# A decode step of attention and feed-forward: sixteen partitions of the first w_down load come through GpSimd's DMA queue

## The chip, the cores and the metric

The kernel runs on one core of a Trainium2 chip. The metric is the device time of one execution in microseconds (us), the median of several runs. The kernel before took 408.2 us, the median of three runs that lie between 408.13 and 408.52 us.

## The reference: what is computed

It is one decode step of a transformer layer for one token. All tensors are bfloat16.

```python
x = A_x                                                     # 1 x 1024
h = x + _A_ref(_layernorm(x), A_k_cache, A_v_cache, A_wq, A_wo)
h2 = h + _B_ref(_layernorm(h), B_w_gate, B_w_up, B_w_down)  # the output, 1 x 1024
# _A_ref: q = x @ wq (32 heads of 128); scores against 65536 cached keys of 4 kv heads,
#         softmax, times the cached values, then @ wo
# _B_ref: (gelu(x @ w_gate) * (x @ w_up)) @ w_down          # 1024 -> 3584 -> 1024
```

The token is one row, so every matrix is read once and used once. The inputs together are 173 MB, nearly all of it the caches.

## The kernel before, in words

**The ring.** All large inputs pass through one SBUF buffer, `ring`, of three slots. A slot holds 65,536 bytes in each of the 128 partitions. The helper `load` (L171) picks the next slot when its offset is 0, or a place within the current slot otherwise, and issues one DMA from SyncE's queue (SP, L178). It waits for whoever read that place last. There are 26 such loads: wq, sixteen halves of a head's keys or values, wo, w_gate, two halves of w_up, and five pieces of w_down. A load of 128 partitions of 64 KB each appears in the trace as 128 packets, one for each partition. They run on 16 DMA engines, eight packets on each, and are followed on each engine by a 4-byte packet that counts up the semaphore. A load has landed when all 16 engines have counted.

**The order of the work.** First come layernorm and q, then for each of the four kv heads the scores of the keys (PE, with transposes on DVE), the softmax and the sums over the values, then wo, the second layernorm, w_gate, w_up, the gelu and w_down. The order on PE, DVE and ACT in the attention part is written by hand: `keep` (L135) ties each operation to the one before it on its engine, through `pe`, `dv` and `ac`. The scheduler orders the rest by data.

**The end.** `wd_v` views w_down as 128 partitions of 28 columns, each column 1024 numbers (2 KB) wide; row f of w_down is partition f // 28, column f % 28. The five loads take 14, 7, 4, 2 and 1 columns, one after another in one slot, which is the slot that wo had. For each column, `out_mm` (L490) multiplies the column of `actz` with the 1024 numbers in four matmuls of 256, into the four groups of 32 partitions of the PSUM tile `f_ps`. So PE uses a load as soon as it has landed, and the last load holds a single column. After some loads `keep_busy` runs a few matmuls whose result nobody reads. At the end DVE copies `f_ps` to `o_fin` (L581), and SP writes it out (L582).

**GpSimd (POOL).** It issues no DMA in the kernel before. Late in the kernel it clears `o2z`, `hnz` and `actz` (L236) and then takes the power in the second layernorm (`ln_rstd`, L225).

Of the kernel before, what the change touches and what calls it, by code (L numbers as in the profile page):

```python
# [11 lines left out]
BF16 = mybir.dt.bfloat16  # L12
# [5 lines left out]
def kernel(  # L18
# [13 lines left out]
    nc = tc.nc  # L32
    P = 128
    D = A_x.shape[-1]
# [53 lines left out]
    top = ctx.enter_context(tc.tile_pool(name="top", bufs=1))  # L88
# [46 lines left out]
    def keep(op, eng):  # L135
        ins = op.ins
        if eng in latest:
            tc.add_manual_dep(ins, latest[eng].name,
                              mybir.DependencyInfo(mybir.DependencyClass.NoSync, mybir.DependencyReason.DATA),
                              reason="order")  # L140
        latest[eng] = ins
        return op
# [4 lines left out]
    def dv(op):  # L147
        return keep(op, "dv")

    def ac(op):  # L150
        return keep(op, "ac")

# [15 lines left out]

    slot = [NSLOT - 1]

    def load(src, off=0):  # L171
        n, w = src.shape[1], src.shape[2]
        if off == 0:
            slot[0] = (slot[0] + 1) % NSLOT
        assert off + n * w <= 2 * CW
        o = slot[0] * 2 * CW + off
        tv = ring[:, o:o + n * w].rearrange("p (n w) -> p n w", w=w)
        nc.sync.dma_start(out=tv, in_=src)  # L178
        return tv

    wq_v = A_wq.rearrange("(p c) n -> p c n", c=DC)
# [1 line left out]
    nc.scalar.dma_start(out=x_row[0:97:32, :], in_=A_x[0, 0].rearrange("(g n) -> g n", g=4))  # L183
    assert DC * HD == 2 * CW
    wq_t = load(wq_v[:])

    make_identity(nc, ident_bf[:])
# [12 lines left out]
    for bp in range(4):  # L200
        s0 = 64 * (bp // 2) + bp % 2
        nc.vector.tensor_copy(out=esel[:, bp, :, :],
                              in_=ident_bf[:, s0:s0 + 63:2].unsqueeze(1).to_broadcast([P, 4, 32]))
# [30 lines left out]
    def padded(i, vec, ncols, name):  # L234
        t = pt_tile(i, [P, ncols, 32], BF16, name)
        nc.gpsimd.memset(t[:], 0.0)  # L236
        nc.vector.tensor_copy(out=t[:, :, 0], in_=vec)
        return t
# [40 lines left out]
    def kv_load(what, g, li, n):  # L279
        t = load((k_v if what == "k" else v_v)[g][:, li * LN:(li + n) * LN, :])  # L280
        for u in range(n):
            state[(what, g, li + u)] = t[:, u * LN:(u + 1) * LN, :]
# [22 lines left out]
    def k_keep(g, li):  # L305
        qk_ps = state.pop(("qk", g, li))
        if li == 0:
            state[("mx", g)] = small.tile([P, NL], F32, name="mx", tag="mx")
        flat = qk_ps[:].rearrange("p k n -> p (k n)")
        if li < NL - 1:  # L310
            sc = low.tile([P, 2 * 512], F32, name="sc", tag=f"sc{li}")
            ac(nc.scalar.copy(out=sc[:], in_=flat))  # L312
            state[("sc", g, li)] = sc[:]
        else:
            state[("sc", g, li)] = flat
        dv(nc.vector.tensor_reduce(out=state[("mx", g)][:, li:li + 1], in_=flat, axis=AX.X, op=ALU.max))  # L316
# [22 lines left out]
    def softmax_exp(g, li):  # L339
        st = state[("vs", g)]  # L340
        pT = pt_tile(li, [P, GPL, TG * rep], BF16, "pT")
        flat = pT[:].rearrange("p m c -> p (m c)")
        ac(nc.scalar.activation(out=flat, in_=state.pop(("sc", g, li)), func=ACT.Exp, bias=st["nbias"][:, 0:1],  # L343
                                scale=scale, accum_out=st["lpart"][:, li:li + 1]))
        st["pT"][li] = pT
# [19 lines left out]
    def v_evac(g):  # L365
        st = state[("vs", g)]
        acc = st["acc"]
        acc_sb = low.tile([P, TG * Dh], F32, name="acc_sb", tag="qk")
        for c in range(4):
            sl = slice(32 * c, 32 * c + 32)  # L370
            if c < 2:
                dv(nc.vector.tensor_copy(out=acc_sb[sl, :], in_=acc[sl, c, :]))  # L372
            else:
                ac(nc.scalar.copy(out=acc_sb[sl, :], in_=acc[sl, c, :]))  # L374
        lsum = small.tile([P, 1], F32, name="lsum", tag="lsum")
        dv(nc.vector.tensor_reduce(out=lsum[:], in_=st["lpart"][:], axis=AX.X, op=ALU.add))
        lrow = small.tile([P, rep], F32, name="lrow", tag="lrow")
        dv(nc.vector.tensor_scalar(out=lrow[:], in0=hmask[:], scalar1=lsum[:, 0:1], scalar2=None, op0=ALU.mult))
        st["end"] = acc_sb, lrow
# [88 lines left out]
    def row_bank(name):  # L468
        return ps_w.tile([P, 512], F32, name=name, tag="w")
# [9 lines left out]
    assert Hq * D == 2 * CW  # L479
    at_ps = [row_bank("at_ps") for _ in range(DS)]  # L480
    wv = load(wo_v[:])
    for c in range(Hq):
        row_mm(at_ps, o2z[:, c, :], wv[:, c, :], c, c < 4, c + 4 >= Hq)
# [6 lines left out]
    def out_mm(stat, mov, first, last, groups=range(4)):  # L490
        for g in groups:
            mm(f_ps[32 * g:32 * g + 32, :], stat, mov(g), first, last, tile_position=(0, 32 * g),
               skip_group_check=True)
# [65 lines left out]
        nc.vector.tensor_tensor(out=by_j(act_bf, j0, nj), in0=src, in1=by_j(gl, j0, nj), op=ALU.mult)  # L559

    wd_v = B_w_down.rearrange("(p c) n -> p c n", p=P)
    sizes = [14, 7, 4, 2, 1]
    assert sum(sizes) == FC
    actz = padded(3, act_bf[:], FC, "actz")
    w_ps = row_bank("w_ps")

    def keep_busy(n, src):
        for _ in range(n):
            mm(w_ps[:], ident_bf[:], src, True, True)

    keep_busy(8, wu[:, 0, 0:512])
    busy = [3, 2, 1, 0, 0]
    c0 = 0
    for sz, nb in zip(sizes, busy):
        wv = load(wd_v[:, c0:c0 + sz, :], c0 * D)
        for cc in range(sz):
            c = c0 + cc
            out_mm(actz[:, c, :], lambda g: wv[:, cc, g * OW:(g + 1) * OW], False, c + 1 == FC)
        c0 += sz
        keep_busy(nb, wv[:, 0, 0:512])  # L580
# [32 lines left out]
```

## Time and profile before

The profile is one execution. Its span, from the first to the last instruction, is 406.4 us. No separate time of that execution is recorded; the median of the runs is 408.2 us, so 1.8 us lie around the span.

| | before |
|---|---|
| median of the runs | 408.2 us (408.13 to 408.52) |
| span of the profiled execution | 406.4 us |
| bytes moved, mean rate | 173.19 MB, 426 GB/s |
| PE busy | 297.6 us (73%) |
| DVE busy | 202.2 us (50%) |
| POOL busy | 7.5 us (2%) |
| last w_down load landed | 402.80 us |
| result copied, write issued | 403.18 us, 403.63 us |

The engines are PE (matrix multiply), PEld (its weight loads), DVE (VectorE), ACT (ScalarE), POOL (GpSimd) and SP (SyncE). A line of the timeline has the start in us, the time taken, the engine, the kernel's line, the operation, its output and inputs, the number of instructions, and in brackets how long the engine stood idle before and what ended that. A row "DMA" gives, for 40 equal slices of the stretch asked for, the mean busy share of the 16 DMA engines in tenths.

The trace also holds a record of each DMA packet: its start, length, bytes and queue, but not the number of its engine. Since an engine starts a packet at once when the one before ends, the packets can be strung into 16 series, end to start. The 16 counts of each load's semaphore are in the trace too, with their times.

### The profile page before, as it was taken

To read this page: it belongs to the slowest core of one execution; us is meant where nothing else is said; L and a number is where in the kernel's file an instruction comes from. 1 tells how busy PE (TensorE), PEld (TensorE's weight loads), DVE (VectorE), ACT (ScalarE), POOL (GpSimd) and SP (SyncE) were. 2 spreads that over 40 slices of the span, in tenths; PEclk is the share of its full clock that TensorE was granted. 3 is DMA by queue.
4 is the path that set the end of the run, shared out by engine and by line. 5 is a ranking of instruction groups with operands and counts; after the bars stand their busy time and mean duration, and the time that the engine had idled before them with its cause. 6 is when DMAs were issued, how large, how long until landed. Compare 5 with 4: busy or idle time off the path is not lost.

```text
span 406.4 us, 2649 instructions
## 1 busy us (share of the span) xinstructions
PE 297.6 (73%) x1493; PEld 65.4 (16%) x743; DVE 202.2 (50%) x185; ACT 40.9 (10%) x63; POOL 7.5 (2%) x17
## 2 busy tenths in 40 slices
PE   0160777658799796879979957998795999666283
PEld 0120111111111110131111003111110211312141
DVE  0210978999838743972595397509843000221110
ACT  1000000013000022100000302000031000100000
POOL 2000000000000000000000000000010000000000
PEclk9995589998899999669999968899899699766979
DMA  9999999999999999999999999999999999999995
GB/s 413 413 413 458 471 408 419 413 485 432 419 421 413 484 426 419 427 419 484 413 419 434 426 471 413 419 441 426 458 419 426 440 432 452 414 420 423 429 420 216
DMA packets 3772, 173.19 MB, mean 426 GB/s; under 512 B 424, under 2 KB 432, under 8 KB 688
## 3 DMA queue, kind: packets, MB, share of 16 engines
q1 hardware_dynamic: 3752, 173.02, 98.6%
q8 instruction: 9, 0.15, 0.1%
q14 instruction: 3, 0.02, 0.0%
q10 hardware_dynamic: 8, 0.00, 0.0%
HBM read 173.02 MB, written 0.00 MB: 426 GB/s over the span
## 4 chain that ended last, share of the span: by engine, by line
PE 47%; DMA 30%; DVE 18%; ACT 3%; issue 1%; SPq 0%; ACTq 0%; DVEq 0%
DMA ring<-in_A_k_cache_dram 20%; PE acc_ps L158 18%; DVE ring L291 12%; DMA ring<-in_B_w_down_dram 10%; PE qk_ps L156 10%; PE qk_ps L158 9%; PE acc_ps L156 6%; DVE mx L316 3%; ACT sc L312 2%; DVE pT L349 2%; PE o_ps L156 1%; PE at_ps L156 1%; PE at_ps L158 1%; DVE acc_sb L372 1%; ACT pT L343 1%
## 5 line engine op out<-in xcount | busy, mean ns | idle before, releaser
L291 DVE STREAM_TRANSPOSE ring<-ring 128x2048 uint32<-128x2048 uint32 x64 | 142.5, 2278 | 33.0 <-DMA ring<-in_A_k_cache_dram 32.9
L156 PE MATMUL qk_ps<-ring,wsel 128*128 128x512 bf16 x256 | 108.6, 424 | 48.7 <-DVE ring L291 29.2
L158 PE MATMUL qk_ps<-ring,wsel 128*128 128x512 bf16 x256 | 108.2, 423 | 0.0
L158 PE MATMUL acc_ps<-ring,pT 128*128 128x512 bf16 x384 | 105.7, 385 | 0.0
L156 PEld LDWEIGHTS <-wsel 128*128 128x128 bf16 x256 | 27.3, 107 | 157.2 <-issue 142.9
L156 PE MATMUL acc_ps<-ring,pT 128*128 128x512 bf16 x128 | 49.3, 385 | 0.0
L316 DVE TENSOR_REDUCE mx<-qk_ps 128x1 f32<-128x1024 f32 x16 | 19.5, 1219 | 28.7 <-ACT sc L312 22.5
L349 DVE STREAM_TRANSPOSE pT<-pT 128x1024 bf16<-128x1024 bf16 x16 | 19.3, 1227 | 23.8 <-ACT pT L343 23.8
L156 PEld LDWEIGHTS <-pT 128*128 128x128 bf16 x128 | 12.9, 100 | 91.3 <-issue 91.2
L312 ACT COPY sc<-qk_ps 128x1024 f32<-128x1024 f32 x12 | 12.1, 1012 | 149.2 <-PE qk_ps L158 149.2
L372 DVE COPY acc_sb<-acc_ps 32x512 f32<-32x512 f32 x8 | 5.3, 667 | 30.1 <-PE acc_ps L158 30.0
L343 ACT ACTIVATE pT<-sc,nbias 128x1024 bf16<-128x1024 f32 x12 | 13.7, 1141 | 45.2 <-DVE nbias L335 42.2
L156 PE MATMUL ln_tot<-ln_s,ones_f 128*128 128x1 f32 x8 | 2.1, 337 | 13.4 <-DVE ln_s L209 11.6
L156 PE MATMUL o_ps<-sel,acc_sb 128*128 128x8 f32 x32 | 7.3, 358 | 5.8 <-DVE rl L386 5.4
L156 PE MATMUL q_ps<-ring,xnz 128*32 128x512 bf16 x32 | 4.4, 528 | 8.9 <-DMA ring<-in_A_wq_dram 8.9
L374 ACT COPY acc_sb<-acc_ps 32x512 f32<-32x512 f32 x8 | 4.6, 577 | 59.2 <-DVE acc_sb L372 59.1
L156 PE MATMUL wu_ps<-ring,hnz 128*32 128x512 bf16 x32 | 4.6, 502 | 7.2 <-DMA ring<-in_B_w_up_dram 7.2
L156 PEld LDWEIGHTS o_ps<-sel,acc_sb 128*128 128x128 f32 x32 | 7.0, 324 | 6.0 <-issue 5.1
L156 PE MATMUL wg_ps<-ring,hnz 128*32 128x512 bf16 x32 | 5.1, 577 | 3.9 <-DMA ring<-in_B_w_gate_dram 3.9
L343 ACT ACTIVATE pT<-qk_ps,nbias 128x1024 bf16<-128x1024 f32 x4 | 4.5, 1113 | 29.8 <-PE acc_ps L158 16.8
L156 PE MATMUL f_ps<-ring,actz 128*32 128x256 bf16 x112 | 4.0, 274 | 4.4 <-DMA ring<-in_B_w_down_dram 4.4
L248 DVE COPY q_ev<-q_ps 128x512 f32<-128x512 f32 x1 | 0.7, 691 | 12.9 <-PE q_ps L158 12.9
(105 smaller groups left out, 88.9 us busy)
## 6 DMA issues: line engine op xcount, KB each, us to landing
ring<-in_B_w_gate_dram SPq DMA_DIRECT2D x1, 7168.0 KB
ring<-in_B_w_up_dram SPq DMA_DIRECT2D x2, 3584.0 KB, 37.1
ring<-in_B_w_down_dram SPq DMA_DIRECT2D x1, 3584.0 KB, 36.4
ring<-in_B_w_down_dram SPq DMA_DIRECT2D x1, 1792.0 KB, 39.0
ring<-in_B_w_down_dram SPq DMA_DIRECT2D x1, 1024.0 KB, 40.6
ring<-in_B_w_down_dram SPq DMA_DIRECT2D x1, 512.0 KB
ring<-in_B_w_down_dram SPq DMA_DIRECT2D x1, 256.0 KB, 41.6
ring<-in_A_k_cache_dram SPq DMA_DIRECT2D x8, 38.2
```

Source lines behind the costliest of these rows:

```text
L156: return pe(t.matmul(out, lhsT=lhsT, rhs=rhs, start=start, stop=stop, tile_position=tile_position, skip_group_check=skip_group_check))
L158: op = t.add_instruction(mybir.InstMatmult(name=nc.get_next_instruction_name(), engine=t.engine, start_tensor_calc=start, stop_tensor_calc ...
L248: nc.vector.tensor_copy(out=dst, in_=src)
L291: dv(nc.vector.transpose(out=kt[:, c * w:(c + 1) * w], in_=kt[:, c * w:(c + 1) * w]))
L312: ac(nc.scalar.copy(out=sc[:], in_=flat))
L316: dv(nc.vector.tensor_reduce(out=state[("mx", g)][:, li:li + 1], in_=flat, axis=AX.X, op=ALU.max))
L343: ac(nc.scalar.activation(out=flat, in_=state.pop(("sc", g, li)), func=ACT.Exp, bias=st["nbias"][:, 0:1], scale=scale, accum_out=st["lpart ...
L349: dv(nc.vector.transpose(out=flat, in_=flat))
L372: dv(nc.vector.tensor_copy(out=acc_sb[sl, :], in_=acc[sl, c, :]))
L374: ac(nc.scalar.copy(out=acc_sb[sl, :], in_=acc[sl, c, :]))
```

## The change

The first w_down load of 14 columns becomes two, of 6 and of 8 columns. The one of 6 columns is made by a new function, `load_apart`: SyncE's queue brings partitions 0 to 111, and GpSimd's queue brings partitions 112 to 127 in three loads of 6, 6 and 4 partitions. Ahead of each of these stands a tiny load into a new tile `turn`, 4 bytes in each of 10 partitions, and after the last one a tiny load for 2 partitions. So GpSimd's queue gets seven DMAs, of 10, 6, 10, 6, 10, 4 and 2 partitions. `po` ties them in this order. `load` gets an argument for the number of partitions. The list `busy` gets a 0 for the added load, so the idle matmuls after the first six columns stay three.

```diff
+    def po(op):
+        return keep(op, "po")
...
-    def load(src, off=0):
+    def load(src, off=0, parts=P):
...
-        nc.sync.dma_start(out=tv, in_=src)
+        nc.sync.dma_start(out=tv[0:parts], in_=src[0:parts])
...
-    sizes = [14, 7, 4, 2, 1]
+    sizes = [6, 8, 7, 4, 2, 1]
...
+    turn = top.tile([P, 2], BF16, name="turn")
+
+    LOW, HIGH = 10, 6
+
+    def load_apart(src):
+        tv = load(src, parts=P - 16)
+        at = P - 16
+        for n in (HIGH, HIGH, 16 - 2 * HIGH):
+            po(nc.gpsimd.dma_start(out=turn[0:LOW, :], in_=A_x[0, 0, 0:2 * LOW].rearrange("(p n) -> p n", n=2)))
+            po(nc.gpsimd.dma_start(out=tv[at:at + n], in_=src[at:at + n]))
+            at += n
+        po(nc.gpsimd.dma_start(out=turn[0:2 * HIGH - LOW, :],
+                               in_=A_x[0, 0, 0:2 * (2 * HIGH - LOW)].rearrange("(p n) -> p n", n=2)))
+        return tv
...
-    busy = [3, 2, 1, 0, 0]
+    busy = [3, 0, 2, 1, 0, 0]
...
-        wv = load(wd_v[:, c0:c0 + sz, :], c0 * D)
+        wv = load_apart(wd_v[:, :sz, :]) if c0 == 0 else load(wd_v[:, c0:c0 + sz, :], c0 * D)
```

In the built program POOL issues the first tiny load after it clears `xnz`, at the start of the kernel. It issues the first load of 6 partitions, the second tiny load and the second load of 6 after it clears `actz` and ahead of `ln_rstd` of the second layernorm. The other three DMAs follow `ln_rstd`. SP's order keeps, with one load more.

## The prediction

> **What bounds the kernel now.** I read the page's row of the DMA engines first, then the queues, then the chain of waits near the end, and last the timeline of the last microseconds.
>
> ```profile
> DMA  9999999999999999999999999999999999999995
> ...
> q1 hardware_dynamic: 3752, 173.02, 98.6%
> q8 instruction: 9, 0.15, 0.1%
> q14 instruction: 3, 0.02, 0.0%
> ```
>
> The 16 DMA engines are busy from the first slice to the last; SP's queue (q1) holds them for 98.6% of the span. PE (73%) and DVE (50%) have room. Two other queues carry twelve small packets called "instruction".
>
> ```profile
> 361.22 41.58 DMA ring<-in_B_w_down_dram
> 402.80 0.04 issue
> 402.84 0.32 PE f_ps L156 x4
> 402.84 0.29 PE L156 MATMUL f_ps<-ring,actz 128*32 128x256 bf16 x4 [0.23 <-DMA ring<-in_B_w_down_dram]
> 403.18 0.42 DVE L581 CAST o_fin<-f_ps 97x256 bf16<-97x256 f32 x1 [11.29 <-PE f_ps L156]
> ```
>
> The first three lines are the chain, the others the timeline. PE waits for the last w_down load, which lands at 402.80; four matmuls, a copy and the write out follow, 3.6 us to the span's end at 406.4. Nothing of the change touches that tail, so the time moves with the last landing.
>
> Now the DMA engines between 400 and 403 us, in slices of 0.075 us:
>
> ```profile
> DMA  9759896959492938383734645554920000000000
> ...
> q1 hardware_dynamic: 243, 0.61, 50.8%
> q8 instruction: 1, 0.02, 2.2%
> ```
>
> They don't end together. The share sinks for over a microsecond before it is 0. The semaphore counts of the last load give it exactly: six engines land within 0.31 us of the first (400.82), one at +0.64, nine from +1.33 to +1.98. The mean of the 16 is 1.06. In the load that lands at 21.8 us all 16 lie within 0.53 us. The packet series show where the lateness comes from. A 64 KB packet takes 2418 ns (27.1 GB/s), thousands of times alike. Each instruction packet delays one engine for good: one of 16 KB at 264.9 us takes 879 ns, and the engine's next packet 2967 instead of 2418, 1.41 us in all; those of 8 KB cost 0.84, 0.55 and 0.84 us. Up to 402 us eight of the former and three of the latter fell on different engines, two of the latter on one: ten are late, six are not.
>
> **The change part by part.**
>
> *SP's part of the first load.* Of 128 partitions 112 stay, seven on each engine for eight. One partition's six columns are 12,288 bytes. The w_down row of 14,336 bytes takes 535 ns, so this row takes 0.46 us. Each engine ends 0.46 us earlier from there on. That the split stays even and at full rate isn't shown: no load of before has 112 partitions. Bounds: seven equal rows (nothing added), or engines hindering each other in pairs through all seven (7 x 0.46 = 3.2 us more). I take the first, as all 26 loads before ran evenly.
>
> *GpSimd's part.* Sixteen rows of 0.46 us come back, three on each of four engines and two on each of two others, if loads of 6, 6 and 4 partitions use as many engines, always from the same six. The tiny loads are there to turn the choice by 10 and 2. No row shows how GpSimd's queue picks engines. The nearest is ACT's load of x at 6.7 us: four partitions, four packets on four engines. If the six are the early ones, the worst of them stands at 0.31 - 0.46 + 3p against 1.98 now, where p is the price of a row. If they are late ones, at 1.98 - 0.46 + 3p.
>
> [...]
>
> *The price p of a row from another queue.* Lower bound: 0.46 us, as on its own queue; ACT's 512-byte packets of x delayed their engines by only 24 ns. Upper bound: the rows of one load come one after another, since they go to neighbouring partitions, and no row of before shows several engines doing that: 6 x 0.46 = 2.76 us a load, 1.84 us the load of four, 7.36 us in all for three rows. The nearest rows in size and in coming from another queue are the instruction packets: 0.74 us for 8 KB in the mean, 1.41 us for 16 KB; midway p = 1.08 us for 12 KB. I take that. [...]
>
> [...]
>
> *The tiny loads* are 4 bytes in 10 partitions. By ACT's packets they delay an engine by some 0.03 us each. From the instruction packets (0.74 at 8 KB, 1.41 at 16 KB) a line back to zero bytes gives 0.07 us: 0.14 us for the two late ones. I take 0, as late engines don't end last in my case; the first tiny load falls at the start and delays ten engines by the same 0.03 us.
>
> *POOL's order.* Three DMA issues now stand ahead of `ln_rstd`, which all of the second layernorm waits for.
>
> ```profile
> 347.93 0.84 POOL L236 MEMSET actz<- 128x896 bf16 x1 [6.60 <-PE acc_ps L158]
> 365.32 0.55 POOL L225 TENSOR_TENSOR ln_rstd<-ln_ve,neg_half 128x1 f32<-128x1 f32 x1 [16.55 <-DVE ln_ve L223]
> 368.94 0.62 PE L156 MATMUL wg_ps<-ring,hnz 128*32 128x512 bf16 x4 [3.90 <-DMA ring<-in_B_w_gate_dram]
> ```
>
> The first waits until PE has read wo's first six columns (about 355.9 us), and `ln_rstd` is due at 365.1: 9 us for three issues. SP's five issues took 3.79 us, 0.76 each; ACT's one 1.08. They hide, up to 3 us each. If that cover went, PE waits for w_gate until 368.94 anyway, and `hnz` is there at 366.4: another 2.5 us. The second tiny load waits for the first, which landed at the start; the third waits behind `ln_rstd` for the second, and the last for the third. Nothing but POOL's end is queued behind them. All rows land in the stages of w_gate and w_up, 20 us ahead of use. There the worst early engine stands at 0.31 + 3 x 1.08 = 3.55 against 1.98 now, since it is spared a row of SP's only afterwards; so the second half of w_up, which landed at 385.82, may land 1.6 us later. That moves the gelu chain and `actz` (391.9 us), hidden by w_down, which streams to 402.80.
>
> *SP and PE.* SP issues one load more (0.76 us), 30 us ahead of the engines' need. PE starts on six columns earlier than on 14; its five waits for w_down (4.4 us in all) show it ahead of the DMA throughout. Neither moves the end. One more count is 9 ns an engine.
>
> *Sum.* High engines: 0.31 - 0.46 + 3 x 1.08 = 3.09; late ones: 1.98 - 0.46 = 1.52. The last landing is at +3.09 instead of +1.98: 403.9, the span 407.5. With the 1.84 us that lie around the span in the median: **409.3 us**, +1.1.
>
> **The rivals.**
>
> *The rows cost what their bytes cost.* Then p = 0.46, the high engines end at 1.23, the late ones at 1.52: 0.46 us earlier, **407.7 us**, -0.11%. For it: x's packets. It is "no change": I call 0.2% (0.82 us) about what a measurement of this kernel tells from no change. Break-even is at p = 0.71; from p = 0.98 the kernel is slower by over 0.2%. So cheap rows of every kind up to 0.98 stay within. A gain over 0.2% needs perfect balance (1.98 - 1.06 = 0.92 us, 407.3), which whole rows can't give.
>
> *The rows of one load hinder each other.* The six rows of a load go to six neighbouring partitions at once, from six engines. At the upper bound the engines end at 0.31 - 0.46 + 7.36 = 7.2: **413.4 us**; at half of it 3.5 (409.8). It decides from 0.25 us a row over the price of its bytes. The six early engines work within 0.31 us of one another, so their rows would meet. Against it: no row of the trace shows such hindering.
>
> *It misses its aim.* The rows fall on late engines: 1.98 - 0.46 + 3 x 0.46 = 2.90, +0.9, **409.1 us**; at p = 1.08 +2.8, 411.0. For it: nothing in the trace names engines.
>
> **How the numbers follow.** Forecast (rows at about the price of instruction packets, 409.0 to 409.9): 0.32. Cheap rows, within 0.2%: 0.30. Rows that hinder each other, or the 112-row part doing so (410 to 413.4): 0.23. Missed aim: 0.10. Faster by over 0.2%: 0.05, for lateness in unprofiled runs that the trace can't show. Slower is 0.32 + 0.23 + 0.10 = 0.65, same 0.30. The range is 407.6 to 412.2: from just under the clean case to well into the third; it leaves out the faster 0.05 and about 0.12 above.
>
> **What would show it.** The 16 counts of the last load: late ones 0.46 us nearer to the first, and four others last. A GpSimd queue whose 12 KB packets take over 0.46 us, or followed by a lengthened packet of q1. Rows in one load that take two or more times 0.46 at once would show the second rival, rows on the series of late engines the third. `ln_rstd` still at 365.3 shows that POOL's issues hide. I am wrong if these packets cost only their bytes.

## The result and the profile after

The changed kernel takes **420.13 us** (median of five runs, 419.63 to 420.72) beside 408.52 us (five runs, 408.13 to 408.77) for the kernel before: a ratio of 1.029, with an interval of 1.0279 to 1.0302, or 11.6 us more. The direction was the likelier one of the forecast, the size was not: 409.3 us was expected, and 420.13 lies far above the range. The span grew from 406.4 to 418.8 us.

From the page of the kernel after, the DMA engines' rows over the whole span and their queues:

```profile
DMA  9999999999999999999999999999999999999992
...
DMA packets 4124, 173.19 MB, mean 414 GB/s; under 512 B 648, under 2 KB 656, under 8 KB 912
...
q1 hardware_dynamic: 3880, 172.82, 97.7%
q0 software_dynamic: 224, 0.20, 0.2%
```

The same 173.19 MB are moved, the engines are "busy" as before, GpSimd's queue (q0) took 0.20 MB and 0.2% of the time of the engines, and yet the mean rate fell from 426 to 414 GB/s. 173.19 MB at 414 instead of 426 GB/s is 11.8 us more: the longer span told as a rate. The busy row doesn't show it: a packet that takes longer for the same bytes counts as busy for all of its time (below, 914 ns in place of 460 at a share of 1.01).

Where it is lost is seen in two stretches. The columns are: the stretch, its length, the busy time of PE, PEld, DVE, ACT and POOL with their numbers of instructions, the granted clock, the DMA engines' busy share, and GB/s. From 386 to 394 us SP's part of the first w_down load passes in the kernel after; from 358 to 372 us the first two of GpSimd's three row loads come, between the rows of w_gate and w_up (the third comes at 375.7 us). The kernel before:

```profile
386.00:394.00 8.00, 6.69 (x43) 2.83 (x28) 1.32 (x4) 0.58 (x1) 0.00 (x0) 0.69 0.96 412
358.00:372.00 14.00, 7.56 (x78) 2.79 (x49) 2.60 (x10) 0.58 (x1) 0.55 (x1) 0.62 0.97 418
```

The kernel after:

```profile
386.00:394.00 8.00, 0.24 (x3) 0.00 (x0) 0.00 (x0) 0.00 (x0) 0.00 (x0) 0.71 1.01 222
358.00:372.00 14.00, 1.51 (x16) 0.97 (x17) 2.33 (x10) 0.33 (x1) 1.65 (x3) 0.65 0.97 361
```

The last two columns are to be read together. From 386 to 394 us the engines are busy throughout and move half the bytes. A packet of 12,288 bytes of SP's takes 914 ns in the median instead of the 460 that it takes in the run with the cut alone (27 GB/s), in 109 of the 112 packets by over 30%. From 358 to 372 us the rate is 14% lower.

The timeline at the end, as it was shown of before:

```profile
414.69 0.83 PE L159 MATMUL f_ps<-ring,actz 128*32 128x256 bf16 x12
415.57 0.42 DVE L598 CAST o_fin<-f_ps 97x256 bf16<-97x256 f32 x1 [14.30 <-PE f_ps L159]
416.02 0.63 SPq L599 DMA_DIRECT2D out_dram<-o_fin  x1
```

The copy starts at 415.57 instead of 403.18. The last load's 16 counts tell how the engines arrived. Their mean went from 401.88 to 411.25 us (+9.4), and the last count from 402.80 to 414.82 (+12.0), as the last engine is now 3.6 us behind the mean and not 0.9. So of the 12.0 us 9.4 are lost by all engines, and 2.6 by uneven ends. After the last landing the tail is as long as it was, within 0.4 us.

### The profile page after: what moved, and what is told of

It reads as the page before. It is cut to its first block, busy times and chain, and to the rows that moved or that the text cites. A ratio compares the mean times of both kernels' runs of the same rounds, so it can differ in the third digit from the quotient of the medians.

```text
span 418.8 us, 2666 instructions
## 1 busy us (share of the span) xinstructions
PE 295.3 (71%) x1495; PEld 63.7 (15%) x743; DVE 202.3 (48%) x185; ACT 40.9 (10%) x63; POOL 11.4 (3%) x24
## 2 busy tenths in 40 slices
DMA packets 4124, 173.19 MB, mean 414 GB/s; under 512 B 648, under 2 KB 656, under 8 KB 912
## 4 chain that ended last, share of the span: by engine, by line
DMA 40%; PE 37%; DVE 18%; ACT 2%; another core or an unknown queue 1%; issue 1%; ACTq 0%
DMA ring<-in_A_k_cache_dram 29%; PE acc_ps L161 15%; DVE ring L294 14%; DMA ring<-in_B_w_up_dram 12%; PE qk_ps L159 6%; PE qk_ps L161 6%; PE acc_ps L159 5%; DVE mx L319 2%; ACT sc L315 1%; PE f_ps L159 1%; DVE pT L352 1%; PE w_ps L159 1%; PE wu_ps L159 1%; PE o_ps L159 0%
## 5 line engine op out<-in xcount | busy, mean ns | idle before, releaser
L159 PE MATMUL qk_ps<-ring,wsel 128*128 128x512 bf16 x256 | 106.8, 417 | 50.8 <-DVE ring L294 31.7
L161 PE MATMUL qk_ps<-ring,wsel 128*128 128x512 bf16 x256 | 106.1, 415 | 0.0
L159 PE MATMUL wu_ps<-ring,hnz 128*32 128x512 bf16 x32 | 5.9, 622 | 12.5 <-DMA ring<-in_B_w_up_dram 12.5
L159 PE MATMUL o_ps<-sel,acc_sb 128*128 128x8 f32 x32 | 5.8, 309 | 5.9 <-DVE rl L389 5.5
L159 PE MATMUL f_ps<-ring,actz 128*32 128x256 bf16 x112 | 6.2, 379 | 4.8 <-DMA ring<-in_B_w_down_dram 4.8
L159 PEld LDWEIGHTS <-hnz 128*32 128x32 bf16 x64 | 3.5, 124 | 30.5 <-issue 25.3
```

What stands on the lines that cost most here:

```text
L159: return pe(t.matmul(out, lhsT=lhsT, rhs=rhs, start=start, stop=stop, tile_position=tile_position, skip_group_check=skip_group_check))
L161: op = t.add_instruction(mybir.InstMatmult(name=nc.get_next_instruction_name(), engine=t.engine, start_tensor_calc=start, stop_tensor_calc ...
```

## The experiments

**Theories.** Ways: it is supposed that partitions that lie side by side share a way in, so that it matters which partitions are written at the same time; the long rows below measure it (29 GB/s for partitions 0 to 3). Queue: GpSimd's queue, with its packets and its tiny loads, holds up the engines. Cut: the cut into 6 and 8 columns, or the odd number of rows, costs the time. Each ratio is against the kernel before on the same chip.

The expectations name theories of their own. In the first four, A says that SP's load of 112 partitions is what is slow, and B that GpSimd's rows are. Later ones speak of neighbours (the ways) and of the queue.

### The cut alone

All 128 partitions of both loads come through SP.

```diff
-    sizes = [14, 7, 4, 2, 1]
+    sizes = [6, 8, 7, 4, 2, 1]
-    busy = [3, 2, 1, 0, 0]
+    busy = [3, 0, 2, 1, 0, 0]
```

> The first load of 14 columns is cut into 6 and 8 columns, all 128 partitions through SyncE, no GpSimd DMA. Theory A (SyncE's load of 112 partitions is what is slow: its 12 KB packets took 0.91 us in the median for 0.46) and theory B (GpSimd's rows are what is slow) both expect no change against before, within 0.3 us. A loss of over 2 us would mean that the cut itself, and neither, is to blame.

408.24 us, ratio 0.9996 (0.9986 to 1.0005). All 128 packets of 12 KB take 460 ns, and from 386 to 394 us the core receives 431 GB/s:

```profile
386.00:394.00 8.00, 7.57 (x70) 3.16 (x54) 1.32 (x4) 0.58 (x1) 0.00 (x0) 0.79 1.01 431
```

The cut is free.

### The 112 partitions without GpSimd

The change, but the other 16 partitions come in a second load of SP's.

```diff
-        for n in (HIGH, HIGH, 16 - 2 * HIGH):
...
+        nc.sync.dma_start(out=tv[at:P], in_=src[at:P])
```

> The 6 columns come as 112 partitions and 16 partitions, both through SyncE, no GpSimd DMA. Theory A: 12 KB packets of the 112 partitions at about 0.9 us again, and 5 to 12 us slower than before. Theory B: packets at about 0.46 us and at most 2 us slower (the load of 16 partitions goes to few groups of partitions).

413.3 beside 408.52 us, ratio 1.0126 (1.0109 to 1.0143): +4.8 us by the medians, 5.1 by the ratio, with nothing on GpSimd. The two stretches:

```profile
386.00:394.00 8.00, 6.31 (x43) 2.74 (x31) 1.32 (x4) 0.58 (x1) 0.00 (x0) 0.63 1.01 231
358.00:372.00 14.00, 6.38 (x82) 2.38 (x49) 2.60 (x10) 0.58 (x1) 0.56 (x1) 0.74 0.96 413
```

The half rate is here again (231 GB/s), the earlier stretch is whole. All engines lose alike: the mean count of the last load is 4.9 us later, and the spread (2.05 us) is that of before. What all packets take beyond their bytes from there on sums up to 75 us, or 4.7 us an engine.

### GpSimd's rows alone

SP loads all 128 partitions. GpSimd's seven DMAs stay as they are, but their rows go to columns 22 to 27 of the same slot, which SP fills again later, so 196 KB more are moved (0.45 us an engine) and overwritten.

```diff
-        tv = load(src, parts=P - 16)
+        tv = load(src)
+        o = slot[0] * 2 * CW + 22 * D
+        sv = ring[:, o:o + 6 * D].rearrange("p (n w) -> p n w", w=D)
-            po(nc.gpsimd.dma_start(out=tv[at:at + n], in_=src[at:at + n]))
+            po(nc.gpsimd.dma_start(out=sv[at:at + n], in_=src[at:at + n]))
```

> All 128 partitions of the 6 columns through SyncE, and besides the seven GpSimd DMAs as in the change, whose 16 rows go to the place of later columns in the same partitions, which SyncE's later loads fill again. 196 KB more are moved than before, 0.45 us. Theory A: at most 1.5 us slower than before, w_up packets at 1.06 us. Theory B: 5 to 11 us slower, with w_gate and w_up packets lengthened as in the change.

413.38 beside 408.52 us, ratio 1.0123 (1.0108 to 1.0138): +4.9 us by the medians, 5.0 by the ratio.

```profile
386.00:394.00 8.00, 2.85 (x28) 0.80 (x15) 0.00 (x0) 0.00 (x0) 0.00 (x0) 0.71 0.98 421
358.00:372.00 14.00, 2.31 (x24) 1.28 (x25) 2.63 (x10) 0.58 (x1) 2.27 (x5) 0.66 0.97 363
```

Now the earlier stretch suffers and the later one is whole. SP's 12 KB packets take 460 ns; instead, at each of GpSimd's three row loads, the packets then under way are lengthened on **all 16** series, those without a row of GpSimd's too, by about 0.64, 0.8 and 1.05 us. The mean count of the last load is 3.5 us later, the last one 5.35.

Each half of the change is so worth about 5 us by itself, together some 9.7 of the 11.6 us (4.8 + 4.9 by the medians; 0.45 less without the 196 KB). Each of the two theories A and B expected the other half to be nearly free, and neither is. The rest, about 2 us, belongs to their being together. The change's own trace says where it lies. SP's packets after 383 us exceed the time of their bytes by 97.9 us in all, 6.1 us an engine, where without GpSimd it was 4.7; and the last engine ends 3.6 us behind the mean, where with GpSimd's rows alone it was 2.7. Why the two halves together cost more, no run shows.

### Loads alone, rows of 12 KB

Behind the end of the kernel before, twelve loads of six columns follow one another, each with nothing beside it.

```diff
+    for q, sl in ((nc.sync, slice(0, 128)), (nc.sync, slice(0, 112)), (nc.sync, slice(0, 96)), (nc.sync, slice(0, 64)),
+                  (nc.sync, slice(112, 128)), (nc.sync, slice(0, 128, 8)), (nc.sync, slice(0, 4)),
+                  (nc.gpsimd, slice(112, 118)), (nc.gpsimd, slice(112, 116)), (nc.gpsimd, slice(0, 96, 16)),
+                  (nc.gpsimd, slice(0, 112)), (nc.gpsimd, slice(0, 128))):
+        nc.sync.dma_start(out=av[:, 0:1, :], in_=alone[:, 0:1, :])
+        q.dma_start(out=av[sl], in_=alone[sl])
```

> The kernel before, with twelve loads of the same 6 columns (12 KB rows) one at a time after its end, each behind a load of 128 partitions and one column. Through SyncE: 128, 112, 96, 64 partitions, the last 16, every eighth, the first 4. Through GpSimd: 6 partitions from 112, 4 from 112, every sixteenth of 96, 112 and 128 partitions. Theory A: 128 partitions 0.46 us a packet, 112 about 0.9 us even alone; if neighbouring partitions share a way in, the last 16 take 4 x 0.46 = 1.8 us a packet and every eighth 0.46 to 0.9 us. Theory B: 112 partitions alone at 0.46 us, GpSimd's loads of 6 and 4 partitions well over 0.46 us. A theory without sharing expects 0.46 us for each packet of every load.

Median packet by SP: 460 ns with 128 partitions, 668 with 112, 804 with 96, 960 with 64. Through GpSimd's queue 460 with 128 and 700 with 112. So fewer partitions cost time on an idle chip and by either queue: that speaks against the queue. (With 96 partitions the number of rows an engine is even, if they are dealt evenly, and the packets take longer than with 112.) The 112 partitions alone were expected at about 900 ns. On four neighbours sharing a way it decides nothing, and what was expected of sharing was missed: 16 neighbouring rows and 16 rows eight apart both took 719 ns in the median, and landed only 0.58 us apart. Through GpSimd's queue six rows side by side took 790 ns and six spread ones 542. Single rows of 12 KB are too short to show more.

### The rows spread out, first try

As the kernel with GpSimd's rows alone, but the rows go to every fourth partition, 3 to 63.

```diff
+        at = 3
-            po(nc.gpsimd.dma_start(out=sv[at:at + n], in_=src[at:at + n]))
-            at += n
+            po(nc.gpsimd.dma_start(out=sv[at:at + 4 * n:4], in_=src[at:at + 4 * n:4]))
+            at += 4 * n
```

> As e3_gpsimd_alone, but the 16 rows of GpSimd go to partitions four apart (3, 7, up to 63) and no longer to 112 to 127. Theory of neighbours (rows that go to the same few partitions at once hold up all engines): the pauses of 0.6 to 1.05 us, which all 16 engines showed at each of the three loads in e3, shrink to under 0.2 us, and the kernel is at most 2 us slower than before, from the 0.45 us of added bytes and three rows on some late engine. Theory of the queue (GpSimd's rows hold up all engines wherever they go): 413.4 us again, within 0.5.

412.69 us, ratio 1.0106 (1.0091 to 1.0121), and **inconclusive**. The spread rows were tied to PE's reads of w_up and issued at 389.65 us, not ahead of `ln_rstd`, and SP's last loads waited for them:

```profile
393.00:396.00 3.00, 2.22 (x51) 1.29 (x44) 0.00 (x0) 0.00 (x0) 0.00 (x0) 1.00 1.02 429
396.00:402.00 6.00, 2.15 (x29) 1.18 (x30) 0.00 (x0) 0.00 (x0) 1.54 (x3) 0.81 0.42 141
```

The time was lost from 396 to 402 us, where the engines stand idle for more than half of it (share 0.42). But from 393 to 396, while the first load of six rows and the start of the second pass, the rate is whole, and no packet beside them is lengthened; these twelve rows take 460 ns each.

### The same rows through ACT's queue

The rows go to partitions 112 to 127, from ACT's queue, without tiny loads; again 196 KB are moved twice.

```diff
-            po(nc.gpsimd.dma_start(out=sv[at:at + n], in_=src[at:at + n]))
+            nc.scalar.dma_start(out=sv[at:at + n], in_=src[at:at + n])
```

> As e3_gpsimd_alone, the same 16 rows to partitions 112 to 127 in loads of 6, 6 and 4, but through ACT's queue and without the tiny loads; no GpSimd DMA. Theory of neighbours: pauses on all engines at each load as in e3, and 2 to 6 us slower than before. Theory of the queue: no pauses, at most 2 us slower (0.45 us of bytes, and three rows more on engines that may be the late ones).

412.58 beside 408.28 us, ratio 1.0104 (1.0087 to 1.0121): +4.3, with the same pauses on all series (0.5 to 0.9 us) and no DMA of GpSimd's. The stretch in which the rows pass:

```profile
358.00:372.00 14.00, 2.96 (x44) 1.18 (x25) 2.59 (x10) 0.58 (x1) 0.55 (x1) 0.72 0.99 355
```

The queue is out as the main cause.

### Loads alone, rows of 57 KB

As before with loads behind the end, now of all 28 columns, 57,344 bytes a row, and with the partitions read and written chosen apart from each other.

```diff
+    for q, sl, so in ((nc.sync, slice(0, 128), slice(0, 128)), (nc.sync, slice(0, 112), slice(0, 112)),
+                      (nc.sync, slice(0, 64), slice(0, 64)), (nc.sync, slice(0, 128, 2), slice(0, 64)),
...
+        q.dma_start(out=av[sl], in_=wd_v[so])
```

> The kernel before, with twelve loads of rows of 28 columns (57,344 bytes, 2.12 us on an unhindered engine) one at a time after its end, with the partitions written and the rows read chosen apart: 128 to 128; 112 to 112; rows 0 to 63 to partitions 0 to 63; rows 0 to 63 to even partitions; even rows to partitions 0 to 63; even rows to even partitions; rows 112 to 127 to partitions 112 to 127; the same rows to every eighth partition; rows 0 to 15 to every fourth partition of 64; 4 rows to 4 partitions; through GpSimd 6 rows to 112 to 117, and the same rows to 3, 7, up to 23. If the partitions written decide, 64 neighbours take about 4.2 us a packet whichever rows are read and even partitions less; if the rows read decide, it is the other way round. If four neighbouring partitions pass no more than one engine's rate, rows 112 to 127 take 8.5 us a packet and 2.12 us when spread; if they pass two engines' rate, 4.2 us.

Each line is a stretch in which one load streams. They write, in this order: partitions 0 to 127; 0 to 111; 0 to 63; the 64 even ones; 112 to 127; every fourth of 0 to 63; 0 to 3:

```profile
405.40:423.70 18.30, 0.00 (x0) 0.00 (x0) 0.00 (x0) 0.00 (x0) 0.00 (x0) 0.50 0.97 401
427.70:454.50 26.80, 0.00 (x0) 0.00 (x0) 0.00 (x0) 0.00 (x0) 0.00 (x0) 0.50 0.96 240
459.00:478.20 19.20, 0.00 (x0) 0.00 (x0) 0.00 (x0) 0.00 (x0) 0.00 (x0) 0.50 0.89 185
482.70:492.80 10.10, 0.00 (x0) 0.00 (x0) 0.00 (x0) 0.00 (x0) 0.00 (x0) 0.50 0.91 363
...
533.70:541.90 8.20, 0.00 (x0) 0.00 (x0) 0.00 (x0) 0.00 (x0) 0.00 (x0) 0.50 0.70 84
...
556.80:561.80 5.00, 0.00 (x0) 0.00 (x0) 0.00 (x0) 0.00 (x0) 0.00 (x0) 0.50 0.80 184
565.80:573.70 7.90, 0.00 (x0) 0.00 (x0) 0.00 (x0) 0.00 (x0) 0.00 (x0) 0.50 0.23 29
```

64 rows to neighbouring partitions come at 185 GB/s, 64 rows to the even ones at 363, with nearly the same busy share. Which rows are read makes no difference (0 to 63 filled from the even rows: 184; the even partitions from the even rows: 378). Four rows to partitions 0 to 3 come at 29 GB/s together, about the 27 of a single engine, with a busy share of 0.23, or 3.7 of the 16 engines. Sixteen rows to every fourth partition of 0 to 63 get 184, about seven engines' rates and not 16, so these rows too are held up; by what, no run shows. Rows 112 to 127 take 7.6 us a packet in their own partitions and 4.3 in every eighth, neither of the pairs of numbers that were expected. And GpSimd's six rows, the same ones both times, take 6686 ns in the median to partitions 112 to 117, 2406 ns to 3, 7, ... 23. So the partitions written decide, by themselves.

### One row an engine, spread or side by side

Two kernels that differ in the partitions of GpSimd's rows, both so that no engine should bring more than one row of a load. The rows read differ with the partitions; that this makes no difference was seen with the loads alone (185 and 184 GB/s). Both: `ring` as three tiles, so that GpSimd's rows wait for nothing new; SP loads all 128; GpSimd's 6, 6 and 4 rows come without tiny loads, 196 KB twice.

```diff
+        sv = rings[(slot[0] + 1) % NSLOT][:, 22 * D:28 * D].rearrange("p (n w) -> p n w", w=D)
+        at = 0
...
+            sl = slice(3 + 4 * at, 3 + 4 * (at + n), 4)     # spread; side by side: slice(P - 16 + at, P - 16 + at + n)
+            po(nc.gpsimd.dma_start(out=sv[sl], in_=src[sl]))
```

> SyncE brings the 6 columns for all 128 partitions. Before that, GpSimd brings 16 rows of 12 KB to the place of later columns, in loads of 6, 6 and 4 without tiny loads, so that each engine gets about one; the rows go to partitions 3, 7, up to 63. The ring is three tiles in place of one, so that nothing else waits for these rows. 196 KB more than before, 0.45 us. Theory of neighbours: no pauses, 0.3 to 0.8 us slower than before. Theory of the queue: 2 us or more slower.

> The same kernel as e8 but for the partitions: GpSimd's 16 rows go to 112 to 127. Theory of neighbours: pauses on all 16 engines at the three loads, 2 to 4 us slower than before and at least 1.5 us slower than e8. Theory of the queue: the same time as e8.

Spread: 410.72 us, ratio 1.006 (1.0045 to 1.0075), +2.4. Side by side: 412.67, ratio 1.0113 (1.0095 to 1.0131), +4.4; its profile is of the slowest of its four runs, 414.07 us. The same stretch of the kernel before, without such rows:

```profile
362.00:365.00 3.00, 1.34 (x16) 0.82 (x7) 1.33 (x6) 0.00 (x0) 0.00 (x0) 0.76 1.01 440
```

The first of the loads, in the spread kernel:

```profile
362.00:365.00 3.00, 0.00 (x0) 0.10 (x1) 0.46 (x2) 0.00 (x0) 1.50 (x3) 0.52 1.00 429
```

and side by side:

```profile
362.00:365.00 3.00, 0.00 (x0) 0.10 (x1) 0.46 (x2) 0.00 (x0) 1.59 (x3) 0.53 1.09 326
```

Six rows spread cost the stream next to nothing there, and no packet beside them is lengthened by 0.15 us; six side by side take a quarter of it. Same queue, same bytes, same number of rows in each load: the 2 us between the two are the partitions'. That the spread kernel still loses 2.4 us where 0.3 to 0.8 was expected is a miss of the expectation. Its trace divides them: the last load's counts are 1.3 us later in the mean, 0.45 of that for the bytes and 0.8 for packets lengthened by its second and third loads (side by side it is 2.8), and 1.1 us are uneven ends. Why its second and third loads still lengthen packets was not separated: they were issued one right behind the other, the same sixteen fours of 0 to 63 passed only 184 GB/s with the loads alone, and what a spread row costs SP's stream beside it was not measured by itself.

### Two halves through SP

The six columns come as partitions 0 to 63 and then 64 to 127: no odd number of rows, no GpSimd.

```diff
+        tv = load(src, parts=P // 2)
+        nc.sync.dma_start(out=tv[P // 2:P], in_=src[P // 2:P])
```

> The 6 columns come through SyncE as partitions 0 to 63 and then 64 to 127, no GpSimd DMA. Theory of neighbours: each half writes only half of the ways in, so the 12 KB packets take about 0.9 us and the kernel is 3.5 to 7 us slower than before, though the load is of a power of two and each engine gets four rows of each half. If only the odd number of 7 rows an engine is to blame for the 112 partitions, no change.

413.24 us, ratio 1.0119 (1.0102 to 1.0135), with packets of 864 ns in the median and 229 GB/s from 386 to 394 us:

```profile
386.00:394.00 8.00, 4.16 (x31) 1.37 (x19) 0.69 (x1) 0.58 (x1) 0.00 (x0) 0.50 1.00 229
```

The half rate is the same as with 112 partitions, though 64 rows are four an engine, if they are dealt evenly. So it needs no odd number of rows, and the cut alone is free.

### The change with rows of half the length

```diff
-    sizes = [6, 8, 7, 4, 2, 1]
+    sizes = [3, 11, 7, 4, 2, 1]
```

> The change with 3 columns in the first load and 11 in the second, so that every row of SyncE's 112 and of GpSimd's 16 partitions has 6 KB and not 12 KB; the number of loads, rows and tiny loads stays. If the loss is bytes written to hindered partitions, about half of it: 4.5 to 7 us slower than before. If it is a price for each load, packet or tiny load, 10 to 12 us again.

413.23 us, ratio 1.0121 (1.0106 to 1.0136): +4.9 where the change has +11.6. With half the bytes in the wrong places the loss is less than half; it is no fixed price of a DMA. In this run `ln_rstd` came behind all of GpSimd's DMAs, at 377.16 us; the loss is still one of the stream, as the last load landed 4.75 us later (407.55).

### The tiny loads alone

The cut, and GpSimd's four tiny loads without the row loads.

```diff
-        tv = load(src, parts=P - 16)
+        tv = load(src)
...
-            po(nc.gpsimd.dma_start(out=tv[at:at + n], in_=src[at:at + n]))
```

> The first load is cut into 6 and 8 columns, all 128 partitions through SyncE, and GpSimd issues only the four tiny loads (4 bytes in 10, 10, 10 and 2 partitions), one after another near the start, while keys stream in. All theories that blame rows or the 112 partitions: no change, within 0.3 us of before. If GpSimd's queue itself, or its small packets on all 16 engines, hold up the stream: over 1 us slower.

408.4 beside 408.42 us, ratio 1.0001 (0.9991 to 1.0011). Without rows to wait for they are issued near the start, so this prices the packets, not their place; but in the kernel with GpSimd's rows alone no packet that starts between 373 and 377 us, where the 4-byte packets of the third tiny load pass, is lengthened by 0.15 us either.

## Why the prediction was wrong, step by step

**The last landing sets the end: right.** The time moved with it, +12.0 us of landing and +11.6 us of time. That it would be later was forecast too, but from the price of instruction packets, which is not what made it later; the direction came out right for another reason than the one given.

**SP's part of the first load: wrong.** The step took "the split stays even and at full rate" as nothing added, "as all 26 loads before ran evenly". All of those wrote 128 partitions, so they said nothing of 112. The bound that was worked out and not taken (3.2 us, engines in pairs through seven rows) is about what the 112 packets show: 53.1 us over their bytes, 3.3 us an engine. Even it was short, since the packets queued behind them are held up as well (of the 97.9 us over the bytes after 383 us, 44.8 are theirs): the kernel without GpSimd lost about 5 us.

**The price p of a row: wrong term.** 1.08 us was taken from instruction packets. GpSimd's rows themselves take 542 ns in the median, near the lower bound, and they exceed their bytes by only 2.5 us all together. But a price a row on its own engine was the wrong kind of term. Six rows, or four, hold up the streams of all 16 engines by 0.6 to 1 us at each load. With GpSimd's rows alone the last load's counts were 3.5 us later in the mean of all engines, 0.45 of it for added bytes, and uneven ends made that 5.35 us for the last. The forecast counted on a loss in q0's packets and in single packets behind them; it stood in q1's, on every engine.

**The rivals.** That cheap rows cost their bytes is refuted. That rows of one load hinder each other was the right mechanism (with the loads alone six rows of 57 KB took 6686 ns side by side and 2406 spread), with 0.23 on it, and its place was too narrow: it was priced for GpSimd's six engines, and the 112 partitions were kept as another, separate unknown. Both came true, and the loads alone speak for one cause, though no run spread the 112 rows differently. The sum of both upper bounds, 3.2 + 5.2 = 8.4 us over the 408.2, would have been 416.6, still short. That engines which bring none of the rows are held up too is in neither.

Why 112 partitions lose so much no run shows. The loads alone give 401 GB/s for 128 partitions and 240 for 112, 29 for partitions 0 to 3 and 184 for sixteen rows to every fourth of 0 to 63.

**The aim.** Whether the rows reached the early engines is not settled. The forecast's sum has three rows on each of four early engines; no run shows this, nor that the tiny loads turn the choice of engines. In the kernel with GpSimd's rows alone they fell on about four early and two late series, but series that lie close can be confused in the stringing. It no longer matters much: the balance could have won at most the 0.92 us that the prediction worked out for a perfect one, against the 11.6 lost.

**What hid, hid.** POOL's issues ahead of `ln_rstd`, on its timeline after:

```profile
354.87 0.55 POOL L578 DMA_DIRECT2D ring<-in_B_w_down_dram  x1 [6.67 <-PE at_ps L161]
355.41 0.52 POOL L577 DMA_DIRECT2D turn<-in_A_x_dram  x1
355.92 0.52 POOL L578 DMA_DIRECT2D ring<-in_B_w_down_dram  x1
361.93 0.57 POOL L228 TENSOR_TENSOR ln_rstd<-ln_ve,neg_half 128x1 f32<-128x1 f32 x1 [5.50 <-DVE ln_ve L226]
```

Three issues of 0.52 to 0.55 us, and POOL then stood idle for 5.5 us until DVE was done. The tiny loads cost nothing, as taken. The second half of w_up, expected up to 1.6 us late, landed 9.7 us late (395.55), which PE's wait shows:

```profile
395.60 0.62 PE L159 MATMUL wu_ps<-ring,hnz 128*32 128x512 bf16 x4 [9.35 <-DMA ring<-in_B_w_up_dram]
```

The gelu chain now ends at 401.3 us, as `actz` is copied, instead of 391.9. It still hides: PE has caught up by 404 us and waits 2.34 us for the next load.

**What stays open.** How SP's queue deals 112 rows to 16 engines (the trace gives no engine numbers), and so which of them meet. Why engines that bring none of the rows also stop, by 0.64 to 1.05 us at each load with GpSimd's rows alone. And why the change exceeds its two halves by some 2 us. No experiment pointed to a version faster than before.

## What to carry to other kernels

Keep loads that stream at full rate at all 128 partitions (401 GB/s for 57 KB rows, 240 with 112 partitions), or, with fewer, try spreading the partitions written over the whole range (64 even ones ran at 363 GB/s, 64 neighbours at 185). Beside a full stream, sixteen neighbouring rows sent aside by GpSimd's or ACT's queue cost 4.3 to 4.9 us where their bytes cost 0.45, and the same rows spread still 2.4. Read the DMA busy share only beside GB/s: a share of 1.0 at half the rate, as here, means packets that take twice as long (914 ns for 460). And when a change puts something in two places that no row of the profile shows, ask whether one mechanism decides both, and add their bounds.

## What the runs showed of the hardware that was not expected

- Four to six rows to neighbouring partitions hold up all 16 engines, also those that bring none of the rows: 0.5 to 1.1 us at each of the small loads, from GpSimd's queue and from ACT's.
- 112 neighbouring partitions are filled at 240 GB/s where 128 are at 401, and 64 neighbouring ones at 185 where 64 even ones are at 363.
- With rows of 57 KB four neighbours get 29 GB/s together, about one engine's 27; with single rows of 12 KB sixteen neighbours landed only 0.58 us later than sixteen rows eight apart.
